# A three-stage fp32 kernel on one core: planned durations set to the trace, and a new table of order and engines

## The chip, the cores and the metric

The kernel runs on one core of a Trainium2 chip. The time is device time in microseconds (us). The kernel before took 601.26 us, the median of three runs (601.25 to 602.89).

## The reference

Three stages follow one another; all tensors are fp32.

```python
# attention: q, k, v of shape (2, 8, 768, 64)
k_sum = k.reshape(B, H, 24, 32, D).max(axis=3)       # a summary of each block of 32 keys
v_sum = v.reshape(B, H, 24, 32, D).mean(axis=3)
scores_l = scale * q @ k.T, kept where |i - j| < 16, else -1e9
scores_s = scale * q @ k_sum.T + log(32)
a = softmax over [scores_l, scores_s]
x = a @ [v, v_sum]                                     # -> 1536 tokens of 512
# first MLP: w_in 512x2048, w_out 2048x512
h = x @ w_in
g = (a0 + a1 h + a2 h^2 + a3 h^3) / (1 + |b0||h| + |b1|h^2 + 1e-6)
x = g @ w_out
# second MLP
h = x @ w_in2;  g = h * cos(h);  out = g @ w_out2
```

## The kernel before

**Work.** The kernel keeps fp32 accuracy on TensorE by splitting operands of the large products into a high and a low part (gh and gl, xH and xL, both halves of a weight tile w) and adding three products: high by high, high by low, low by high. L777 makes a low part (value minus high part), L324, L322 and L327 are the copies and casts on POOL (GpSimd), ACT (ScalarE) and DVE (VectorE); one helper serves each engine, so their lines appear under many tiles.

**Attention.** K of the first batch comes in by pairs of heads (L454), TensorE transposes it (L463, tile ktp), a copy takes it out of PSUM (tile big) and DVE reduces each block to its maximum (L471). Q is transposed likewise (L432 for the first tile, L581 later, tile qtp; the copy goes to qT). For each tile of 128 queries the key windows are gathered into a tile room; L626 computes scores (tile sp, two halves of the tokens' heads in two PSUM tiles, so two tile numbers alternate); L656 on DVE adds the mask, scales and takes the row minimum, one operation (shown as two instructions) for each pair of heads; L660 on ACT takes the exponential and the row sum; L670 and L673 normalise; L687 transposes the weights (ptp to pt); L734 multiplies with the values (avp). L495 is the block maximum for the second batch, whose K tiles L489 transposes.

**The MLPs.** Weights arrive as 64-bit words and DVE rebuilds fp32 from them by integer operations (L760, L764, L768), a tile of 128 x 512 at a time. L864 is the first h product. L1013 to L1041 evaluate the rational function on ACT, DVE and POOL; L1023 is one product in it. L962 is the second h, L1057 to L1069 the cosine. L1106 accumulates the outputs in PSUM (acc), and L1150, L1136, L1159 finish and store them. The accumulators are saved and refilled by copies (acc<-room, room<-acc, part<-acc).

**What sets the order.** The program first lists operations (`P.op`), each with the engines that can do it and a planned duration on each, then `Plan.order` unpacks a table, `ORDER`, which names for each place in the program the operation and its engine. Every engine runs its instructions in that order, and the DMAs that SP (SyncE) issues stand in the table too. The planned durations (the pairs such as `("T", 0.78)` for TensorE, S for SP) set nothing in the built program beside the table: they were the inputs with which the table was found. Dependencies between operations give the waits. So a change of table moves instructions and can change the engine of an elementwise operation; it can't change what is computed.

Of the kernel before, what the change touches and what calls it, by code (L numbers as in the profile page):

```python
# [17 lines left out]
AX = mybir.AxisListType  # L18
# [3 lines left out]
QC = 1.0 + 1e-6  # L22
# [13 lines left out]
for _p, _t in (("AA", .143), ("AP", .17), ("AT", .25), ("AV", .14), ("PA", .08), ("PP", .08), ("PT", .15),  # L36
# [203 lines left out]


def pool(n):
    return Shared(0.2 + n * 0.00207)


MM = 0.2275
SPT = 1.2


@with_exitstack  # L250
def kernel(
    ctx: ExitStack,
# [26 lines left out]
    G = 4  # L279
# [1047 lines left out]
```

## Time and profile before

| | us |
|---|---|
| median of three runs | 601.26 |
| the profiled execution's span, first to last instruction | 599.4 |
| around the span (median minus span) | 1.9 |
| TensorE (PE) busy | 585.9 (98%) |
| DVE busy | 548.4 (92%) |
| ACT busy | 434.1 (72%) |
| POOL busy | 304.3 (51%) |

The profile is a single execution, and its times are counted from the span's start. PE is matmul, PEld the weight load beside it, SPq the queue from which SP issues DMAs. In a timeline a row joins neighbouring instructions of one line, and its bracket says how long the engine had been idle before, and what ended that. The clock that TensorE was granted is 1.00 in every stretch shown.

### The profile page before, as it was taken

To read this page: it belongs to the slowest core of one execution; us is meant where nothing else is said; L and a number is where in the kernel's file an instruction comes from. 1 tells how busy PE (TensorE), PEld (TensorE's weight loads), DVE (VectorE), ACT (ScalarE), POOL (GpSimd) and SP (SyncE) were. 2 spreads that over 40 slices of the span, in tenths; PEclk is the share of its full clock that TensorE was granted. 3 is DMA by queue.
4 is the path that set the end of the run, shared out by engine and by line. 5 is a ranking of instruction groups with operands and counts; after the bars stand their busy time and mean duration, and the time that the engine had idled before them with its cause. 6 is when DMAs were issued, how large, how long until landed. Compare 5 with 4: busy or idle time off the path is not lost.

```text
span 599.4 us, 10933 instructions
## 1 busy us (share of the span) xinstructions
PE 585.9 (98%) x3897; PEld 501.0 (84%) x3897; DVE 548.4 (92%) x1119; ACT 434.1 (72%) x954; POOL 304.3 (51%) x303
## 2 busy tenths in 40 slices
PE   8879999999999999999999999999999999999997
PEld 7568878888888888888888888888989989998996
DVE  4999999979999999998999999999999998887874
ACT  3989999877587756876789897766767566554653
POOL 5587975247537564557577542444355423732130
PEclk9999999999999999999999999999999999999999
DMA  9897874200321313311220112123322331100104
GB/s 264 218 258 192 204 209 120 75 0 2 106 71 37 106 36 105 106 52 56 70 71 1 36 36 71 37 71 104 109 71 70 106 108 36 35 1 1 53 1 158
DMA packets 68862, 51.85 MB, mean 87 GB/s; under 512 B 37304, under 2 KB 63160, under 8 KB 68808
## 3 DMA queue, kind: packets, MB, share of 16 engines
q1 hardware_dynamic: 68664, 51.03, 29.0%
q8 instruction: 30, 0.49, 0.3%
q14 instruction: 24, 0.20, 0.1%
q10 hardware_dynamic: 144, 0.13, 0.1%
HBM read 47.71 MB, written 3.15 MB: 85 GB/s over the span
## 4 chain that ended last, share of the span: by engine, by line
PE 87%; DVE 9%; ACT 2%; DMA 1%; issue 0%; POOL 0%; SPq 0%; POOLq 0%; DVEq 0%; ACTq 0%
PE acc L1106 43%; PE h L864 22%; PE h L962 18%; DVE sc L656 2%; DMA vw<-in_v_dram 1%; PE avp L734 1%; DVE f L764 1%; DVE f L768 1%; PE ptp L687 1%; PE sp L626 1%; PE warm L356 1%; PE ktp L463 1%; DVE f L760 1%; PE vmp L542 0%; DVE big L471 0%
## 5 line engine op out<-in xcount | busy, mean ns | idle before, releaser
L1106 PE MATMUL acc<-gh,w 128*128 128x512 f32 (+1 forms) x416 | 123.1, 378 | 0.0
L1106 PE MATMUL acc<-w,gh 128*128 128x512 f32 x382 | 119.3, 394 | 0.0
L864 PE MATMUL h<-xH,w 128*128 128x512 f32 (+1 forms) x320 | 99.1, 371 | 0.1
L777 POOL TENSOR_TENSOR gl<-te,gh 128x512 fp32r<-128x512 f32 (+1 forms) x48 | 62.7, 1307 | 67.2 <-ACT gh L322 33.5
L1106 PEld LDWEIGHTS acc<-gh,w 128*128 128x128 f32 x416 | 75.3, 188 | 14.9 <-issue 1.5
L1106 PE MATMUL acc<-gl,w 128*128 128x512 f32 (+1 forms) x208 | 77.6, 373 | 0.0
L1106 PEld LDWEIGHTS acc<-w,gh 128*128 128x128 f32 x382 | 66.7, 189 | 9.4
L1106 PE MATMUL acc<-w,gl 128*128 128x512 f32 x191 | 74.3, 389 | 0.0
L1023 POOL TENSOR_TENSOR tu<-tu,tf 128x512 f32<-128x512 f32 (+1 forms) x41 | 51.4, 1255 | 41.2 <-ACT tf L1015 40.9
L777 POOL TENSOR_TENSOR w<-f,w 128x512 fp32r<-128x512 f32 x39 | 54.4, 1397 | 29.5 <-ACT w L322 15.0
L864 PEld LDWEIGHTS h<-xH,w 128*128 128x128 f32 x320 | 58.5, 188 | 10.6 <-DVE big L495 0.3
L864 PE MATMUL h<-xL,w 128*128 128x512 f32 (+1 forms) x160 | 58.9, 368 | 0.0
L864 PE MATMUL h<-big,w 128*128 128x512 f32 x216 | 52.0, 389 | 0.0
L768 DVE SCALAR_TENSOR_TENSOR f<-raw,f 128x512 int32<-128x512 int32 x64 | 48.3, 759 | 0.3
L1013 ACT ACTIVATE tu<-h,co 128x512 f32<-128x512 f32 (+1 forms) x52 | 33.9, 652 | 19.3 <-PE h L864 18.2
L764 DVE SCALAR_TENSOR_TENSOR f<-raw,f 128x512 int32<-128x512 int32 x64 | 47.3, 745 | 0.6
L864 PEld LDWEIGHTS h<-big,w 128*128 128x128 f32 x216 | 40.6, 188 | 8.4
L1106 PEld LDWEIGHTS acc<-gl,w 128*128 128x128 f32 x208 | 39.1, 188 | 7.0
L1106 PEld LDWEIGHTS acc<-w,gl 128*128 128x128 f32 x191 | 35.9, 188 | 7.9
L1057 ACT ACTIVATE tu<-te 128x512 int32<-128x512 f32 x27 | 17.1, 632 | 32.5 <-DVE te L987 32.2
L324 POOL TENSOR_SCALAR w<-f 128x512 fp32r<-128x512 f32 x28 | 20.0, 715 | 39.8 <-DVE f L768 35.1
L1033 ACT ACTIVATE h<-tf 128x512 f32<-128x512 f32 (+1 forms) x52 | 29.6, 570 | 12.0 <-DVE te L1027 10.8
(222 smaller groups left out, 1530.9 us busy)
## 6 DMA issues: line engine op xcount, KB each, us to landing
raw<-in_moe_w_in_dram SPq DMA_DIRECT2D x32, 512.0 KB, 4.6
raw<-in_moe_w_out_dram SPq DMA_DIRECT2D x32, 512.0 KB, 3.4
vw<-in_v_dram SPq DMA_DIRECT2D x24, 192.0 KB, 3.5
qk<-in_q_dram SPq DMA_DIRECT2D x10, 256.0 KB, 5.3
out_dram<-part SPq DMA_DIRECT2D x8, 256.0 KB, 2.8
part<-in_k_dram SPq DMA_DIRECT2D x8, 192.0 KB, 4.8
big<-in_v_dram SPq DMA_DIRECT2D x3, 512.0 KB, 6.7
qk<-in_k_dram SPq DMA_DIRECT2D x6, 256.0 KB, 5.4
```

The costliest lines, as they stand in the source:

```text
L324: nc.gpsimd.tensor_scalar(out=o, in0=i, scalar1=1.0, scalar2=1.0, op0=ALU.mult, op1=ALU.mult)
L656: lambda e, pr=pr, hh=hh, sv=sv, sp=sp: nc.vector.tensor_tensor_reduce(out=sv()[:, pr, :], in0=sp.t[:, pr, :], in1=m.t, op0=ALU.add, op1=A ...
L764: lambda e: nc.vector.scalar_tensor_tensor(out=ft.t.bitcast(I32), in0=lohi()[1], scalar=-0x40000000, in1=ft.t.bitcast(I32), op0=ALU.bitwis ...
L768: lambda e: nc.vector.scalar_tensor_tensor(out=ft.t.bitcast(I32), in0=lohi()[0], scalar=29, in1=ft.t.bitcast(I32), op0=ALU.logical_shift_r ...
L777: lambda e: E[e].tensor_tensor(out=lo(), in0=x(), in1=hi().bitcast(F32), op=ALU.subtract),
L864: nc.tensor.matmul(out=h.t[:, 0:n], lhsT=lt, rhs=rt[:, kk, cs], start=(k0 == 0 and i == 0), stop=(k0 == 2 and i == 5))
L962: nc.tensor.matmul(out=bank.t[:, c], lhsT=lt, rhs=rt, start=start and i == 0, stop=stop and i == 5, skip_group_check=True)
L1013: lambda e: nc.scalar.activation(out=U(), in_=H(), func=ACTF.Square, scale=b1s))
L1023: lambda e: E[e].tensor_tensor(out=U(), in0=U(), in1=Z(), op=ALU.add))
L1033: lambda e: nc.scalar.activation(out=H(), in_=Z(), func=ACTF.Exp, scale=-1.0))
L1057: lambda e: nc.scalar.activation(out=K().bitcast(I32), in_=S_(), func=ACTF.Identity, scale=1.0 / (2.0 * math.pi)))
L1106: nc.tensor.matmul(out=dst, lhsT=lt, rhs=rt, start=(un.start and not have and i == 0), stop=(un.stop and i == 2), skip_group_check=have)
```

## The change

No operation is added or removed: TensorE has 3421 matmuls and SP 142 issues either way. Some eighteen planned durations are set to other values, which by themselves set nothing in the program, and the table is replaced. Its text is unreadable; a line of it stands for the rest.

```diff
 ORDER = (
-    "c-rk)ON?g6RsQOA-*w;jf4}<g{`)o4-P7Zq=^1+-9?wi>?7=wWB#vccTP8ROa%>aJ1|csTD`5dy#8QX>i%1qqK!CD{;t"
+    "c-rk*TaP8zRbKm6wd;OAb?V&voIaO6eL3CJJ>#CtxSh;+7`yGs#P$T65U?F^BqA;b;uwS#WRQ|zDJY0I5)YP~2ozA1AfzZ#q"
...
-MM = 0.2275
-SPT = 1.2
+MM = 0.2267
+SPT = 0.98
...
-            P.op([("S", 0.62)], [], [raw],
+            P.op([("S", 0.58)], [], [raw],
...
-            P.op([("T", 0.78)], [raw], [tp], tr)
+            P.op([("T", 0.67)], [raw], [tp], tr)
...
-        P.op([("T", 0.44)], [raw], [tp], tr)
+        P.op([("T", 0.36)], [raw], [tp], tr)
...
-            P.op([("T", 0.44)], ss, [pp], tr)
+            P.op([("T", 0.355)], ss, [pp], tr)
...
-            P.op([("T", 6 * 0.12)], reads, [bank[half]] + ([hx["b"]] if wn == "11" else []), mm)
+            P.op([("T", 6 * 0.1185)], reads, [bank[half]] + ([hx["b"]] if wn == "11" else []), mm)
```

What the table does is seen in the order of instructions on an engine. Some fifty elementwise operations change engine: DVE makes 22 of the low parts gl<-te where it made 31, POOL 49 where it made 40; L1023 goes from 11 to 6 on DVE and from 41 to 46 on POOL; DVE gets 7 of the high casts of weights (w<-f) that POOL had, and 6 refills of accumulators that ACT had.

**The first matmuls.** On PE at the program's start, before: ktp are transposes of K, qtp of Q, sp scores.

```order
L356 MATMUL warm<-ident 128x128 x8
L463 MATMUL ktp<-ident,part 64x128 x12
L432 MATMUL qtp<-ident,part 64x64 x16
L463 MATMUL ktp<-ident,part 64x128 x30
L432 MATMUL qtp<-ident,part 64x64 x8
L626 MATMUL sp_290<-room,qT_214 64x120
L626 MATMUL sp_292<-room,qT_214 64x120
```

And the same place now:

```order
L356 MATMUL warm<-ident 128x128 x8
L463 MATMUL ktp<-ident,part 64x128 x24
L432 MATMUL qtp<-ident,part 64x64 x16
L463 MATMUL ktp<-ident,part 64x128 x24
L432 MATMUL qtp<-ident,part 64x64 x8
L626 MATMUL sp_308<-room,qT_234 64x120
L626 MATMUL sp_310<-room,qT_234 64x120
```

Twelve more transposes of K stand ahead of the first sixteen of Q, and all 48 are issued before the first score; before, six were left until after the first four scores. To match, SP now issues the small load of the coefficients first, then four parts of K, then both of Q (before: two of K, one of Q, one of K, one of Q).

**The first scores on DVE.** Before, the block reductions (L471) and one sum of values (L514) stand ahead of most of the scores (L656, each with a second instruction that writes mn), and behind them stands a long run of scores:

```order
L656 ISA mn 128x1
L514 TENSOR_TENSOR big<-big 128x8x64
L471 TENSOR_REDUCE big<-ktp 128x12 x2
L656 ISA sc,mn<-sp_290,room 128x120
L656 ISA mn 128x1
L656 ISA sc,mn<-sp_292,room 128x120
L656 ISA mn 128x1
L656 ISA sc,mn<-sp_290,room 128x120
```

Now the reductions are all done before the first score, a copy of qT, which the next scores on PE need, stands amid the scores, and L514 comes twelve scores later:

```order
L471 TENSOR_REDUCE big<-ktp 128x12 x2
L656 ISA sc,mn<-sp_310,room 128x120
L656 ISA mn 128x1
L656 ISA sc,mn<-sp_308,room 128x120
L656 ISA mn 128x1
L656 ISA sc,mn<-sp_308,room 128x120
L656 ISA mn 128x1
L656 ISA sc,mn<-sp_310,room 128x120
L656 ISA mn 128x1
L392 RECIPROCAL co<-co 128x1
L656 ISA sc,mn<-sp_308,room 128x120
L656 ISA mn 128x1
```

The scores of one PSUM tile are now taken as soon as the matmuls that fill it are issued, not after them all.

**The last elementwise work on DVE.** tu and te are values of the second MLP, gh and gl their parts. Before:

```order
L327 CAST gh<-te 128x512
L1061 SCALAR_TENSOR_TENSOR h<-tu,h 128x512
L777 TENSOR_TENSOR gl<-te,gh 128x512
L1069 TENSOR_TENSOR tu<-tu,h 128x512
L327 CAST gh<-tu 128x512
L777 TENSOR_TENSOR gl<-tu,gh 128x512
L327 COPY room<-acc_6862 128x512
L327 COPY room<-acc_6875 128x256
```

And now:

```order
L327 CAST gh<-te 128x512
L1061 SCALAR_TENSOR_TENSOR h<-tu 128x512
L1061 SCALAR_TENSOR_TENSOR h<-tu,h 128x512
L1069 TENSOR_TENSOR tu<-tu,h 128x512
L327 CAST gh<-tu 128x512
L327 COPY room<-acc_6843 128x512
L327 COPY room<-acc_6856 128x256
```

Both last low parts have left DVE; they stand at the end of POOL's order.

## Rows read from the trace of the kernel before

**Rows 1.** The page: span, busy time of each engine, chain of waits.

```profile
span 599.4 us, 10933 instructions
...
PE 585.9 (98%) x3897; PEld 501.0 (84%) x3897; DVE 548.4 (92%) x1119; ACT 434.1 (72%) x954; POOL 304.3 (51%) x303
...
PE 87%; DVE 9%; ACT 2%; DMA 1%; issue 0%; POOL 0%; SPq 0%; POOLq 0%; DVEq 0%; ACTq 0%
```

**Rows 2.** Busy time by stretch: length, PE, PEld, DVE, ACT, POOL, clock, DMA.

```profile
0.00:20.00 20.00, 16.85 (x244) 13.66 (x244) 11.09 (x45) 9.28 (x35) 11.25 (x39) 1.00 0.94 262
20.00:40.00 20.00, 15.92 (x223) 12.07 (x222) 19.77 (x78) 19.33 (x75) 12.95 (x14) 1.00 0.87 218
40.00:50.00 10.00, 9.23 (x138) 7.89 (x139) 10.00 (x45) 9.01 (x36) 7.12 (x9) 1.00 0.93 249
50.00:100.00 50.00, 48.31 (x582) 41.04 (x582) 48.39 (x177) 47.36 (x166) 38.75 (x43) 1.00 0.73 192
100.00:590.00 490.00, 490.00 (x2689) 421.93 (x2688) 456.96 (x774) 347.53 (x645) 234.21 (x202) 1.00 0.19 59
590.00:600.00 10.00, 5.59 (x28) 4.44 (x26) 2.24 (x4) 1.55 (x3) 0.00 (x0) 1.00 0.28 105
```

**Rows 3.** Waits of PE, whole span: line, releaser, us in total, times, longest.

```profile
PE warm L356 <- POOL ident masks.py:199: 1.4, 1, 1.4
PE sp L626 <- ACT room L322: 1.0, 1, 1.0
PE qtp L581 <- DVE te L1041: 1.0, 1, 1.0
```

**Rows 4.** Timelines of PE and DVE, 4 to 22 us: start, length, instruction, idle before.

```profile
4.79 0.42 PE L356 MATMUL warm<-ident 128*128 128x128 f32 x1
...
8.66 0.51 PE L432 MATMUL qtp<-ident,part 64*64 64x64 f32 x10 [0.59 <-ACT qT L322]
...
10.20 1.21 DVE L327 COPY big<-ktp 128x384 f32<-128x384 f32 x2 [1.61 <-PE ktp L463]
...
17.49 0.88 PE L626 MATMUL sp<-room,qT 64*64 64x120 f32 x16 [1.03 <-ACT room L322]
...
18.07 0.28 DVE L656 CUSTOM_DVE_ANT_0 sc<-sp,room 128x120 f32<-128x120 f32 x1 [0.19 <-PE sp L626]
...
18.28 0.28 DVE L656 CUSTOM_DVE_ANT_0 sc<-sp,room 128x120 f32<-128x120 f32 x1
```

**Rows 5.** Groups of DVE by line and shape: busy us, mean ns, idle before.

```profile
L777 DVE TENSOR_TENSOR gl<-te,gh 128x512 fp32r<-128x512 f32 x31 | 21.5, 693 | 0.3
...
L1023 DVE TENSOR_TENSOR tu<-tu,tf 128x512 f32<-128x512 f32 x10 | 7.1, 711 | 0.0
```

**Rows 6.** Groups of POOL by line and shape.

```profile
L777 POOL TENSOR_TENSOR gl<-te,gh 128x512 fp32r<-128x512 f32 x40 | 55.8, 1395 | 67.1 <-ACT gh L322 33.5 <-DVE gh L327 13.3 <-PE h L962 10.7
...
L1023 POOL TENSOR_TENSOR tu<-tu,tf 128x512 f32<-128x512 f32 x34 | 45.4, 1336 | 39.4 <-ACT tf L1015 39.1
```

**Rows 7.** Line L764, ns least, median, most; then POOL and DVE from 338 us.

```profile
L764 DVE SCALAR_TENSOR_TENSOR f<-raw,f x64: 678/688/1223, 23.2 to 525.5; 128x512 int32<-128x512 int32 x64
...
338.49 1.28 POOL L777 TENSOR_TENSOR gl<-te,gh 128x512 fp32r<-128x512 f32 x1 [0.90 <-PE h L864]
...
339.09 1.22 DVE L764 SCALAR_TENSOR_TENSOR f<-raw,f 128x512 int32<-128x512 int32 x1
```

**Rows 8.** Timeline of the end, 575 to 600 us.

```profile
582.97 0.28 PE L962 MATMUL h<-big,pt 128*128 128x256 f32 x1
...
590.58 0.69 DVE L777 TENSOR_TENSOR gl<-tu,gh 128x512 fp32r<-128x512 f32 x1
...
595.31 0.28 PE L1150 MATMUL acc<-w,gl 128*128 128x256 f32 x1
...
595.70 0.42 DVE L327 COPY room<-acc 128x256 f32<-128x256 f32 x1 [1.49 <-PE acc L1150]
...
596.40 0.38 SPq L1159 DMA_DIRECT2D out_dram<-room  x1
```

More of the change, by code (lines that the diff above doesn't have):

```diff
@@ new lines @@
+    "yvL-=m_pTP4b&l!%~gFMYr9b5|V9zIk89B|kt--BaNz@LLR?%#cI|JhgX?%#d_>sxDpPs8%X^Bc>(<@x#fM`CgK<mTd;%>@8"
+    "E*j&!Oyni@5nC<VK{Mq{FGx!*m%l)05o!xhLzB8MC`}D7G{)z{`rpKd;mtK4M9NvF?e&g_^+pnJtKfHN%ba;4j|Gs+<j*gtq"
+    "LDMXn`3vrEs#^-?^6})wvK(Jdp0A#%%8UN`Q|mqG7pJ|Vn02SOi@NTN&u-lw6`k{{D2|FlfWJIB>eSh)dNf;A*>btN=$E5xa"
+    ">St1%aSC4`giKpY`3mrK7O{GxW%Bl7!*aG*O3cJaTc7$H;x_H6b~L02Zu@S-3xvrI(cL1{a5HM;O^|T*Jd-<+nmZH$Nj?Q(b"
+    "s23qs!UeXf<-51@M%PzM}j36SqV4)NQ5YgW!v@b8?5j`QdRC9XZaILg$;w2mZ<zVMocPk)5wP4~NAd*SQozy%cG!8ueVE65$"
@@ new lines @@
+    "tx1n#=-U0#2zo9G+Ct&)e46aFdxbwA?s_;c@0^IYHId~u>qR2F$lmrJD<a`mh`-~FrK=l#LAzSYe8O8l1OLi~3*Y~CNAbj4l"
+    "XaJY4{Ne_zCPEnpL4q2T4NBqTk`tO_7YRTA~CG33oZv(Lle(;53e*(P@{Ho(Lph|!|5i$}{1mNE~6O5hUJ=o9k=k{a@%cqg&"
+    "pA0YJodFLz!*WnbUh$A0CW#lj(ah~@&H*-94Ctx^+zjcn6Gh`q;C<-5{kF&cRRjF91M20u0{Gd_evaQ*IX``a!%u#~12gIxe"
+    ")vP&^v*v(_9f)3{N7|Dp%*lOkzvLPeW&;YcO4Z1I~D#b@G`HD06I|1j>G|39HN`2{TnxUpf}y4pyDNms$!|LS~(1catJ%qK5"
+    "Jl)u~V#+!f{-ODHT4Q+)b34sj12}1K`WJ7xkK^aU2Im37hm~&N*AJ**`WtKz2TkaO5KZB;H352Gt(=pGz4hZjAXDNGOG<Yb}"
@@ new lines @@
+    "b*P28`5@+Scgq^x|e1SetKnNC%D!sH*J-|xJ0;P}9`d>K+H<RcM6G=xjW9z6W~1LGybx>Yj$Abl)QZz3T?&-1%oz0Wa8a7P5"
+    "fN7MrU1vYZsvtQDER~1=NXvOwe90+k!cp4s^@E49RkH-K*3`*s2P$N*QmB8)z&`WeT=HdPU@9jB0hxHoe2@y64NX9CLgM$dN"
+    "u<K+&)tQ2vlrkTL|DyY~kCd(Am~)=WB>53^V-HYwe&EC`{yu;j;t*2w`l4}bq<vLRwazogi6B>sC)rp1!skMVF%Kq=eg`vj="
+    ")pc?4pKqn@=fs(%ANOlS3}QxwT2HqsJr+?DUrRXRKi2i?RMXNmskF0Kg*x2JkTygqn%GXZ(Rmx!h2myx7*FMn_fs+R2M12dv"
+    "-JA9xzwu#|>L|b0>#a;XKLn0>;5WY#`wG!hM{;RO$j`nUh^$=6xR@aQCc+8?MWkn#~mRSCiNWk56YCB&i0MA*<&?o}KN~qKc"
@@ new lines @@
+    "%#lvzt<(oF)-q>9o?oUx%>TP+^c6KD%EN9^OaAIP>|2oB3Y(`>Cov`Gc(wzj_z&Zgmsww7o|VKdYgsoj8CUE?J4ZGWK-B(At"
+    "f5Vg`^?pm@@^JOGd_OY-%+NRFdfkl;4BTSRwB$QW9Fp9>em0vMYiuOp-PPGZ;wo$gB5||i|b;rWb>6ejA*fPb0FYS6^<;*bM"
+    "dPy+b0<Z@P(<1G8s}&wPuTady4HGXVyHzZ{6)`%$T`|%G%37h?mcK0sdqg9px05*&tx{0c@|FXnbL~OIHYiRAwUS9mf^E47d"
+    "oZ$1UTo`dE9{mZ0@?;haM@EK-yUjcJ?+PB8*I-_(#FXwnzru9KBwbr3lGIj2Rs`I;nG&wRmZ1<3bxHFYs0pE*Tl}PtXsijtx"
+    "{6Hg;hJz9?z(FY(Q-ZSy5+n!lJ5a3$T?_GE2;awl3th^N6;NC8I87aW#x0OQvT?1A(OTiTocXiy;m"
@@ L515, in v_mean0 @@
                                                    op=ALU.add))
-            P.op([("T", 0.89)], [raw], [vp],
+            P.op([("T", 0.955)], [raw], [vp],
                  lambda e, i=i, x=x: nc.tensor.matmul(
@@ L720, in attn_c @@
                      prio=P.now - lead)
-            P.op([("S", 1.09)], [], [vw["w"]],
+            P.op([("S", 0.87)], [], [vw["w"]],
                  lambda e, vw=vw, w=ws[half]: nc.sync.dma_start(
@@ L737, in mm @@
                             rhs=pts[hh].t[0:KW, pr, c0:c0 + 64], start=True, stop=True)
-        P.op([("T", 1.1)], pts + [vw[x] for vw in vw2 for x in "mw"], [op], mm)
+        P.op([("T", 1.08)], pts + [vw[x] for vw in vw2 for x in "mw"], [op], mm)
         T, c = divmod(128 * u, TT)
```

90 lines of the change are left out of this document (35 added, 55 removed).

## The prediction

> **What bounds the kernel now.** I read the page first: TensorE is busy for 585.9 of a span of 599.4 us and holds 87% of the chain of waits, DVE 9% [rows 1]. A mean like that hides where the other 13.5 us are, so the next view is busy time by stretch [rows 2]. From 100 to 590 us PE is busy for all of 490.00 us. Nothing that the change does there can gain; it can only open a gap. The idle time lies in front and at the end: 3.15 us up to 20 us, 4.08 from 20 to 40, 0.77 from 40 to 50, 1.69 from 50 to 100, and at the end 4.41 in the last ten microseconds, of which 0.6 lie past the span. In front DVE is busy for 19.77 of 20 us between 20 and 40, for all 10.00 from 40 to 50, and 48.39 of 50 after: while PE waits, DVE works without a gap, so DVE carries the front even where the list of PE's waits names ACT, for ACT waits for DVE. That list [rows 3] shows no single step that would be the cure: behind the first matmul's own 1.4 us the longest waits are 1.0 us each, one for ACT's room and one for DVE's te. Last I read the two timelines of the beginning and the one of the end [rows 4, 8].
>
> So the question is small. The execution profiled has 599.4 us of span, and with the 1.9 us around it that is the median of 601.26. All that could go is the idle time in front, 9.7 us, and of that the first matmul's 1.4 stays [rows 3]. What a measurement of this kernel can tell from no change is about 0.3%, or 1.8 us.
>
> **The change part by part.** Same operations, so the PE work in the sum is unchanged; what moves is who waits.
>
> *First transposes.* Before, the transposes of Q stand on PE behind the first twelve of K and wait 0.59 us for ACT, and DVE behind them sits idle 1.61 us until the next ktp arrives [rows 4]. With 24 transposes of K first, DVE has its next pieces at hand. It can't gain more than the 1.61 us; stepping by hand through the arrivals of the K parts I get 0.9 us, nearest to the middle of 0 and 1.61, and I take that. The coefficients' load, now first on SP, delays each K part by one issue; the warm-up matmuls hide that for the first, the last of them starting at 4.79 us [rows 4]. If the part came later than they end, its delay would show whole, one issue, 0.38 us by the row of the last store [rows 8]; between 0 and 0.38 I take 0.
>
> *First scores.* Here the new order may lose. A score operation on DVE that has to wait for its matmuls comes at most 0.58 us after they began: PE starts the run at 17.49, the waiting score starts at 18.07, and the one behind it 0.21 us later [rows 4]. Before, a long run of scores stood behind the reductions, and matmuls had run ahead of it: one wait of 0.19. Now I find four places where PE must wait for a score or for the copy of qT before its next matmuls, and DVE in turn for those. If nothing overlaps, each round takes 0.58 us plus a hop back of about 0.11 (PE's last matmul ends at 595.59, DVE's copy starts at 595.70, [rows 8]) plus 0.21 for the operation, less the 0.06 of a matmul that runs meanwhile (16 in 0.88): 0.84 us, and four take 3.4. Against the 0.9 us won above that is +2.5 us of DVE time. If PE runs ahead as it did before, nothing is lost and DVE stays 0.9 us ahead. The row of before says that a wait can be as small as 0.19, the other end assumes four full rounds; between −0.9 and +2.5 I take the middle, +0.8. Nothing covers a loss here, as DVE has next to no idle time from 20 us on [rows 2].
>
> *Through the front.* How much later than PE's own work PE runs is set by the DVE work that must precede its matmuls. Adding up mean durations along each order, the tightest early place is the 199th row of DVE's order, a block maximum of the second batch (L495): before PE's work of 46.3 us may go on, DVE must have done 56.1 us before and 56.9 now. That is +0.8 us if DVE is the bound there, and it is [rows 2]. Ends: 0, if PE's next wait takes it up, and +0.8. I take +0.8. From PE work 74 us on the new order asks 1 to 3 us less of DVE. Then the later waits lose their reason: PE's idle time of 0.77 and 1.69 us between 40 and 100 us, 2.46 together [rows 2]. Ends −2.46 and, as some of these waits name ACT and POOL, −1.7. I take −2.1.
>
> *The middle.* DVE loses nine low parts of 693 ns and five products of 711, 9.8 us, to POOL, where they take 1395 and 1336, 19.2 us [rows 5, 6]; some casts and refills come to DVE in return. POOL was busy for 304.3 us [rows 1], and PE is without idle time there: worth 0, bounded by 0 and by one late operation, 0.7 us (1.395 less 0.693), as each such part now ends that much later. The nearest gate between a part and its use is the last, so I price it there.
>
> What POOL does beside DVE is not free: the conversion L764 takes 688 ns as a median and 678 at least, yet 1223 at most, on one and the same shape; the longest, from 339.09 us, lies beside a low part on POOL that began at 338.49 and took 1.28 [rows 7]. The Trainium skill (GPSIMD Engine Reference, 8. Key points) says that GpSimd shares its SBUF interfaces with VectorE and that they contend where a DVE instruction has two SBUF inputs or runs in a 2-port mode; the trace agrees in this one pair of rows. By that rule the added work would lengthen some of DVE's operations. Even if all of the 19 us slowed DVE by the ratio 1223 to 688, DVE would lose 19.2 × 0.44 = 8.4 us over 490 us in which it had 33 us idle [rows 2]; the end would not move.
>
> *The end.* The last h is ready about 2 us of PE work later than before, and the last low part takes POOL's 1.4 us in place of DVE's 0.69. Before, the last h matmul ended at 583.25 and the last low part at 591.27 [rows 8], 8.0 us. Now the part itself takes 0.70 more, and the cast and low part of te no longer stand in its way on DVE; by hand the chain takes 7.4 to 7.5 us, and 7.5 to 7.7 us of PE work stand ahead of its use. Cost 0 to 0.7; I take 0.15. The last store hangs on the same kind of copy as before, 0.42 us after 595.70 and issued at 596.40: 0.
>
> Sum: 0.8 + 0.8 − 2.1 + 0.15 = −0.35 us. Against the median of 601.26 that is 600.9.
>
> **The rivals.**
>
> *The front comes out faster.* DVE wins the 0.9 us of the start, the scores cost nothing, and the waits from 40 to 100 us go: −0.9 + 0.8 − 2.46 = −2.6, so 598.7. For it: DVE is the bound and later places ask less of it. If half of the 4.08 us of idle time between 20 and 40 us goes too, 596.7. Against it: the place at PE work 46.3 asks for more.
>
> *The scores go back and forth.* Slower: four full rounds, +2.5, carried whole by a DVE without idle time up to PE work 46.3, +0.8, while of the later waits only 0.9 us goes as DVE is late: +2.4, and with the end +0.3, 604.0. It decides if DVE ends its first block of scores more than about 1.5 us later than my sum has it. For it: PE and DVE wait for each other in the order itself. Against it: the matmuls of a score are short, and PE had 3.15 us idle up to 20 us that can absorb some.
>
> *The end or the middle stalls.* The low parts on POOL come late: +0.7 once at the end, and once or twice in the middle, 602.0 to 602.7. Against it: the other distances are over a microsecond. It stays within what can't be told from no change.
>
> *The table changes nothing that matters.* PE-bound for 490 us, and a front bound by the same DVE work: within 0.5 us of 601.3. I count this with my forecast, since gains and losses that cancel look the same in time.
>
> **How the numbers follow.** Forecast, with gains and losses cancelling to within 1.8 us: 0.47, by itself 599.5 to 603.0. Faster front: 0.30, nearly all of it past the 0.3%. Back and forth: 0.18, all of it slower. A stall at the end or in the middle: 0.05, of which 0.02 slower by more than 0.3%. That gives faster 0.30, same 0.50, slower 0.20. The range takes in the faster case down to 597.6, halfway between its two times, and the slower one up to its lesser half, 603.6.
>
> **What would show it.** In the profile of the changed kernel: DVE's idle time ahead of its second copy of ktp falls from 1.61 us to under 0.8; DVE's first block of scores has waits on PE of some tenths of a microsecond each, adding up to 1 to 3 us, where there was 0.19; PE's busy time in 50 to 100 us is above 49.5 where it was 48.31; 100 to 590 us shows PE busy throughout; POOL's busy time is above 315 and DVE's below 545. The forecast is wrong if PE has idle time after 100 us, which would mean that a low part on POOL or an accumulator's refill comes late; if the stretch from 20 to 50 us loses much less or more than its 4.85 us; or if the last store is issued more than 1 us later after PE's last matmul than 1.09 us.

## The result, and the profile after

The changed kernel takes 605.32 us, the median of four runs (604.06 to 607.16), against 601.25 of before (599.93 to 602.89, four runs): a ratio of 1.007, 95% interval 1.005 to 1.0089. It is slower, by 4.1 us, and above the range of the prediction, 597.6 to 603.6. The rival in which the scores go back and forth, 604.0, lies nearest.

The page of the kernel after, the lines that answer to [rows 1]:

```profile
span 604.2 us, 10965 instructions
...
PE 588.3 (97%) x3897; PEld 502.9 (83%) x3897; DVE 544.6 (90%) x1102; ACT 428.5 (71%) x955; POOL 322.9 (53%) x319
...
PE 83%; DVE 8%; ACT 3%; DMA 3%; issue 1%; SPq 1%; DVEq 0%
```

The span is 4.8 us longer. PE is busy for 2.4 us more although its matmuls are the same 3897, and the chain of waits has lost four points of PE. More busy time for the same work is the first sign that some of it ran slower. Busy time by stretch (columns as in [rows 2]), kernel after:

```profile
0.00:20.00 20.00, 14.98 (x241) 12.62 (x242) 8.53 (x37) 8.86 (x30) 11.08 (x41) 0.96 0.91 262
20.00:40.00 20.00, 17.57 (x226) 12.54 (x224) 18.92 (x84) 19.02 (x70) 11.62 (x11) 0.96 0.77 197
40.00:50.00 10.00, 7.69 (x81) 6.62 (x85) 9.43 (x36) 6.93 (x24) 6.81 (x8) 0.66 0.91 246
50.00:100.00 50.00, 47.88 (x620) 40.67 (x611) 45.36 (x180) 45.96 (x171) 33.23 (x37) 1.00 0.69 177
100.00:590.00 490.00, 489.90 (x2702) 421.97 (x2697) 457.39 (x763) 343.57 (x656) 257.25 (x221) 1.00 0.20 61
590.00:610.00 20.00, 10.33 (x49) 8.45 (x47) 4.98 (x10) 4.12 (x8) 2.93 (x2) 0.98 0.18 67
```

From 100 to 590 us PE is busy for 489.90 us, where it was 490.00 [rows 2]: the middle costs 0.1. At the end it ran 5.59 us before and 10.33 now, so 4.74 us of its work were still to do at 590 us. Less the 0.1, 4.6 us were lost ahead of 100 us. Two things stand out there. Up to 20 us PE is busy for 14.98 where it was 16.85. And the clock, in the third column from the end, was 1.00 in each of these stretches and is 0.96, 0.96 and 0.66 now.

Waits of PE in the kernel after (columns as in [rows 3]):

```profile
PE sp L626 <- DVE mn L656: 2.2, 4, 0.7
PE sp L626 <- ACT qT L322: 1.7, 2, 0.9
PE qtp L581 <- ACT qT L322: 1.7, 1, 1.7
...
PE ktp L463 <- DMA part<-in_k_dram: 0.9, 1, 0.9
```

The first row isn't in the list of before at all. Matmuls of scores wait for reductions of scores, and these wait for matmuls in turn; DVE's waits in the kernel after:

```profile
DVE sc L656 <- PE sp L626: 4.6, 11, 0.9
```

Five of the eleven, 2.7 us, lie among the first sixteen scores, those of the first two tiles of queries. The same row in the kernel before:

```profile
DVE sc L656 <- PE sp L626: 0.5, 2, 0.3
```

PE's timeline of the first scores, kernel after:

```profile
15.02 0.43 PE L626 MATMUL sp<-room,qT 64*64 64x120 f32 x6 [0.50 <-DVE mn L656]
...
16.60 0.85 PE L626 MATMUL sp<-room,qT 64*64 64x120 f32 x24 [0.69 <-DVE mn L656]
18.03 0.52 PE L626 MATMUL sp<-room,qT 64*64 64x120 f32 x8 [0.59 <-DVE mn L656]
19.02 0.68 PE L626 MATMUL sp<-room,qT 64*64 64x120 f32 x8 [0.47 <-DVE mn L656]
```

And DVE's, of the same stretch:

```profile
14.67 0.28 DVE L656 CUSTOM_DVE_ANT_0 sc<-sp,room 128x120 f32<-128x120 f32 x1
...
15.49 0.28 DVE L656 CUSTOM_DVE_ANT_0 sc<-sp,room 128x120 f32<-128x120 f32 x1 [0.53 <-PE sp L626]
...
18.58 0.28 DVE L656 CUSTOM_DVE_ANT_0 sc<-sp,room 128x120 f32<-128x120 f32 x1 [0.70 <-PE sp L626]
...
19.78 0.28 DVE L656 CUSTOM_DVE_ANT_0 sc<-sp,room 128x120 f32<-128x120 f32 x1 [0.91 <-PE sp L626]
...
22.07 0.28 DVE L656 CUSTOM_DVE_ANT_0 sc<-sp,room 128x120 f32<-128x120 f32 x1
```

Read the two side by side. DVE's reduction ends at 18.58 less 0.70, so at 17.88; PE's next eight matmuls start at 18.03; DVE's next reduction starts at 18.58, 0.55 later; PE starts again at 19.02. Each waits for the other. The last row is the sixteenth score. In the kernel before it started at 20.11:

```profile
20.11 0.28 DVE L656 CUSTOM_DVE_ANT_0 sc<-sp,room 128x120 f32<-128x120 f32 x1
```

Why does a matmul wait for a reduction of other heads? The plan's dependencies are by pair of heads: the matmuls write `sp[y]`, the reduction of pair `pr` reads `sp[pr]`. But the four pairs lie in one PSUM tile, and the waits that the program is built with are by tile. In the plan a matmul of the second pair may run while the first is being reduced; on the chip the trace shows it waiting for that reduction. That the sharing of the tile is what makes it wait was tried (below, two tiles).

The clock, in stretches of one microsecond, kernel after:

```profile
18.00:19.00 1.00, 0.52 (x8) 0.25 (x9) 0.29 (x2) 0.00 (x0) 0.16 (x1) 0.63 1.03 341
19.00:20.00 1.00, 0.98 (x9) 0.48 (x10) 0.22 (x3) 0.00 (x0) 0.00 (x0) 0.50 1.16 292
...
42.00:43.00 1.00, 0.96 (x4) 0.66 (x4) 1.00 (x4) 0.99 (x4) 0.88 (x2) 0.57 1.10 336
43.00:44.00 1.00, 0.10 (x1) 0.00 (x0) 1.00 (x4) 0.97 (x5) 1.00 (x2) 0.50 0.95 219
...
48.00:49.00 1.00, 1.00 (x7) 1.00 (x6) 1.00 (x9) 0.51 (x2) 0.38 (x1) 0.51 0.87 188
```

0.50 is the lower of the two levels, 1.2 GHz. In narrower stretches it is seen to hold from about 18.3 to 21.7 us and from about 42.1 to 49.0. The first fall lies amid the score waits. Ahead of the second, PE had stood still for 1.68 us; a second idle place, of 0.93 us, lies inside the slow stretch. PE's timeline, kernel after:

```profile
41.33 0.66 PE L581 MATMUL qtp<-ident,qk 128*128 128x128 f32 x4 [1.68 <-ACT qT L322]
42.04 1.06 PE L489 MATMUL ktp<-ident,qk 128*128 128x128 f32 x4
44.03 1.89 PE L626 MATMUL sp<-room,qT 64*64 64x120 f32 x32 [0.93 <-ACT qT L322]
```

What the lower clock does to a matmul is seen on L517 (ns least, median, most), kernel after; the most is 1061, and was 610 of the same six before (second row):

```profile
L517 PE MATMUL vmp<-big,vsel x6: 592/682/1061, 19.6 to 22.8; 128*24 128x512 f32 x6
...
L517 PE MATMUL vmp<-big,vsel x6: 592/592/610, 18.3 to 21.2; 128*24 128x512 f32 x6
```

At the end of the kernel after, the last matmul starts at 600.05 and the last store is issued 1.11 us later, which was 1.09 [rows 8]:

```profile
600.05 0.28 PE L1150 MATMUL acc<-w,gl 128*128 128x256 f32 x1
...
601.16 0.41 SPq L1159 DMA_DIRECT2D out_dram<-room  x1
```

So there are two candidates for the loss, both in front: the waits between scores and their reductions, and a TensorE clock that fell twice.

### The profile page after: what moved, and what is told of

Its sections match the earlier page's. It is cut to its first block, busy times and chain, and to the rows that moved or that the text cites. A ratio compares the mean times of both kernels' runs of the same rounds, so it can differ in the third digit from the quotient of the medians.

```text
span 604.2 us, 10965 instructions
## 1 busy us (share of the span) xinstructions
PE 588.3 (97%) x3897; PEld 502.9 (83%) x3897; DVE 544.6 (90%) x1102; ACT 428.5 (71%) x955; POOL 322.9 (53%) x319
## 4 chain that ended last, share of the span: by engine, by line
PE 83%; DVE 8%; ACT 3%; DMA 3%; issue 1%; SPq 1%; DVEq 0%
PE acc L1106 39%; PE h L864 23%; PE h L962 16%; DMA vw<-in_v_dram 2%; PE ptp L687 1%; ACT sc L660 1%; PE sp L626 1%; DVE h L1061 1%; PE avp L734 1%; DMA part<-in_k_dram 1%; PE vmp L517 1%; DVE gl L777 1%; DVE f L768 1%; DVE te L1069 1%; PE ktp L463 0%
## 5 line engine op out<-in xcount | busy, mean ns | idle before, releaser
L777 POOL TENSOR_TENSOR gl<-te,gh 128x512 fp32r<-128x512 f32 (+1 forms) x57 | 75.8, 1331 | 48.5 <-ACT gh L322 24.0
L864 PE MATMUL h<-xH,w 128*128 128x512 f32 (+1 forms) x320 | 99.9, 372 | 0.3 <-DVE big L495 0.2
L1023 POOL TENSOR_TENSOR tu<-tu,tf 128x512 f32<-128x512 f32 (+1 forms) x46 | 56.4, 1229 | 40.4 <-ACT tf L1015 38.6
L777 POOL TENSOR_TENSOR w<-f,w 128x512 fp32r<-128x512 f32 x40 | 56.6, 1418 | 39.7 <-ACT w L322 22.3
L864 PEld LDWEIGHTS h<-xH,w 128*128 128x128 f32 x320 | 58.6, 188 | 11.0 <-DVE big L495 0.4
L864 PE MATMUL h<-xL,w 128*128 128x512 f32 (+1 forms) x160 | 58.9, 368 | 0.0
L864 PE MATMUL h<-big,w 128*128 128x512 f32 x216 | 52.4, 389 | 0.0
L1013 ACT ACTIVATE tu<-h,co 128x512 f32<-128x512 f32 (+1 forms) x52 | 33.9, 653 | 23.2 <-PE h L864 21.7
L768 DVE SCALAR_TENSOR_TENSOR f<-raw,f 128x512 int32<-128x512 int32 x64 | 47.3, 742 | 0.5
L864 PEld LDWEIGHTS h<-big,w 128*128 128x128 f32 x216 | 40.6, 188 | 8.4
L764 DVE SCALAR_TENSOR_TENSOR f<-raw,f 128x512 int32<-128x512 int32 x64 | 45.8, 719 | 0.5
L1064 ACT ACTIVATE h<-h 128x512 f32<-128x512 f32 x48 | 28.2, 587 | 21.1 <-DVE h L1061 20.6
L660 ACT ACTIVATE sc<-sc,mn 128x120 f32<-128x120 f32 x96 | 36.9, 387 | 4.3 <-DVE mn L656 4.2
L1035 DVE SCALAR_TENSOR_TENSOR tu<-tu,h 128x512 f32<-128x512 f32 (+1 forms) x52 | 33.4, 641 | 6.4 <-ACT h L1033 5.1
```

Of the source, the lines that this page charges most:

```text
L660: lambda e, pr=pr, hh=hh, sv=sv: nc.scalar.activation(out=sv()[:, pr, :], in_=sv()[:, pr, :], func=ACTF.Exp, scale=-1.0, bias=mn.t[:, hh, ...
L764: lambda e: nc.vector.scalar_tensor_tensor(out=ft.t.bitcast(I32), in0=lohi()[1], scalar=-0x40000000, in1=ft.t.bitcast(I32), op0=ALU.bitwis ...
L768: lambda e: nc.vector.scalar_tensor_tensor(out=ft.t.bitcast(I32), in0=lohi()[0], scalar=29, in1=ft.t.bitcast(I32), op0=ALU.logical_shift_r ...
L777: lambda e: E[e].tensor_tensor(out=lo(), in0=x(), in1=hi().bitcast(F32), op=ALU.subtract),
L864: nc.tensor.matmul(out=h.t[:, 0:n], lhsT=lt, rhs=rt[:, kk, cs], start=(k0 == 0 and i == 0), stop=(k0 == 2 and i == 5))
L1013: lambda e: nc.scalar.activation(out=U(), in_=H(), func=ACTF.Square, scale=b1s))
```

## Experiments

The table can't be edited by eye, but it can be taken apart: the operations up to some place from the one table, and those that remain in the order of the other. For such kernels the edit says which come from where. Ratios are to the kernel before, on the same chip.

**Front of before, rest of after.** The first 848 places are those of the kernel before (its windows follow that kernel's to 100 us: PE busy for 48.35 us from 50 to 100, where before has 48.31; only from 20 to 40 it has 14.95 for 15.92, with a wait of 1.2 us for a load of q that the profile of before lacks), and the later ones come from the kernel after:

```diff
-ORDER = the table of after
+ORDER = the first 848 of before, then what remains, as it stands in after
```

> The table is the order of before for its first 848 operations (up to the last product with the values, about 124 us) and the order of after for the rest. Theory A (the loss lies in the front: scores and matmuls that wait for each other, and a clock that falls where PE sat idle): as before, 600.5 to 602.5 us, clock 1.00 throughout. Theory B (the loss lies in the rest: low parts moved to POOL, the two gaps of 0.2 us at 404 and 408 us and the end): 604 to 606 us.

Measured: 602.11 us, ratio 1.0012 (0.9996 to 1.0029). It can't be told from the kernel before. The new order of the middle and of the end, with the low parts on POOL, costs little: by the interval at most 1.7 us. The two profiles also show that one and the same front can differ by about 1 us from one execution to another.

**Front of after, rest of before.** The reverse, cut at place 837:

```diff
-ORDER = the table of after
+ORDER = the first 837 of after, then what remains, as it stands in before
```

> The reverse: the first 837 operations in the order of after, the rest in that of before. Theory A: as after, 604 to 606 us, with granted clock 0.5 for some microseconds around 20 and 45 us. Theory B: 600.5 to 602.5 us.

Measured: 606.98 us, ratio 1.009 (1.0069 to 1.0111). The loss lies in the first 837 places, but this kernel loses more than the kernel after, for its seam adds a wait that neither whole kernel has (PE's L864 waits 1.67 us at 130.6 us for DVE's L745). Its six runs fall in two groups: 604.41 and 604.55 at a granted clock of 1.0 as the mean over the run, 606.87 to 608.09 at 0.991 to 0.994. The kernel before, at 0.999 or more on the same chip, took 600.92 as a median of 17 runs. So there is a loss of 3.6 us (604.5 less 600.9) without any clock lost, of which the seam can have up to 1.7, and one of 2.4 to 3.6 more in runs with a lower clock. In the kernel after itself the run at 0.999 took 604.06, those at 0.992 605.88 and 607.16. The mean clock has to be read with care: it takes in the very end of the span, where PE is done, so start of after, rest of before (below) has a mean of 0.997 with 1.00 in every stretch up to 590 us.

**Scores of before, rest of after.** To part the start from what follows, the first 117 places (first transposes and first scores) from before:

```diff
-ORDER = the table of after
+ORDER = the first 117 of before, then what remains, as it stands in after
```

> Only the first 117 operations (up to the end of the first block of scores, about 22 us) are in the order of before, all others in that of after. Theory A1 (the first block of scores alone makes the loss, and what comes later follows from it): 600.5 to 602.5 us. Theory A2 (the stretch of 30 to 60 us has a loss of its own, DVE and ACT orders there): 602.5 to 604.5 us, PE idle again about 2.5 us between 39 and 44 us and the clock down there.

Measured: 609.04 us, ratio 1.0126 (1.0107 to 1.0144). This one tells nothing on the question, for the seam itself made a new wait: PE's transposes L687 wait 5.9 us for a normalisation on POOL (L673) that now stands behind other work, and from 20 to 40 us PE is busy for 12.61 us only, at a clock of 0.83.

**Scores behind their matmuls.** The table of after, with only the reductions (L656) and exponentials (L660) of the first two query tiles moved behind the last score matmul of their tile. PE's and ACT's own orders stay as they are; what changes is which matmuls come behind a reduction of their tile in the program. On DVE, the kernel after with minus, this one with plus:

```
 L471 TENSOR_REDUCE big<-ktp 128x12 x2
+L392 RECIPROCAL co<-co 128x1
+L327 COPY qT_317<-qtp 128x256
 L656 ISA sc,mn<-sp_310,room 128x120
...
-L392 RECIPROCAL co<-co 128x1
 L656 ISA sc,mn<-sp_308,room 128x120
 L656 ISA mn 128x1
-L327 COPY qT_317<-qtp 128x256
```

> The table of after with one thing moved: the 28 or so score reductions and exponentials of the first two query tiles that stood between the score matmuls of their tiles stand behind the last of these matmuls. Theory A1 (PE and DVE wait for each other because each reduction of a PSUM tile stands between matmuls into the same tile): PE's waits on the scores, 2.2 us in 4 places, go to nearly none, and the time falls by 1.5 to 4 us, to 601.5 to 604. Theory A2: the waits at the scores go, yet the time falls by under 1 us, since DVE waits for all matmuls first or the later stretch decides.

Measured: 602.56 us, ratio 1.0023 (1.0011 to 1.0036): 2.8 us of the 4.1 are back. At a clock of 1.0 its runs took 600.85 and 600.91, as fast as the kernel before, and the one at 0.999, which is the one profiled, 602.26. PE's waits in this kernel begin with

```profile
PE sp L626 <- ACT qT L322: 2.1, 2, 1.3
PE qtp L581 <- ACT qT L322: 1.5, 1, 1.5
```

and the row with mn is gone. DVE starts its first score later, at 16.08 instead of 14.67 us, and its sixteenth at 20.36 instead of 22.07:

```profile
16.08 0.28 DVE L656 CUSTOM_DVE_ANT_0 sc<-sp,room 128x120 f32<-128x120 f32 x1
...
20.36 0.28 DVE L656 CUSTOM_DVE_ANT_0 sc<-sp,room 128x120 f32<-128x120 f32 x1
```

Starting each score as soon as it can start costs 1.7 us by the sixteenth. Both falls of the clock are missing from this profile: it is 1.00 in every stretch up to 590 us.

**Scores in two PSUM tiles.** The order of after untouched; the four pairs of heads of the first two query tiles lie in two PSUM tiles in place of one:

```diff
+        alt = [new("pa", [128, NP, KW], F32, f"acc{[(1, 2), (0, 3)][u][hh]}", 1, f"sp{hh}") for hh in range(2)] if u < 2 else sps
+        spt = lambda hh, pr: (alt if (u < 2 and (pr % 2 if u == 0 else pr > 1)) else sps)[hh].t
...
-                            nc.tensor.matmul(out=sps[hh].t[c0:c0 + 64, pr, :],
+                            nc.tensor.matmul(out=spt(hh, pr)[c0:c0 + 64, pr, :],
...
-                         out=sv()[:, pr, :], in0=sp.t[:, pr, :], in1=m.t, op0=ALU.add, op1=ALU.min,
+                         out=sv()[:, pr, :], in0=spt(hh, pr)[:, pr, :], in1=m.t, op0=ALU.add, op1=ALU.min,
```

> The table of after, unchanged; only the scores of the first two query tiles go to two PSUM tiles for each half of the heads where they shared one, so that a matmul of one pair of heads need not wait for the reduction of another pair. Theory A1 (the waits come from sharing the tile, not from the data): the waits of the score matmuls on DVE's reductions, 2.2 us in 4 places, fall to under 1 us with the same order, and the time falls by 1 to 3 us against after's 605.3, to 602.5 to 604.5. Rival (DVE and PE need each other's data in that order): the waits stay, 604.5 to 606.5.

Measured: 603.79 us, ratio 1.0032 (1.0018 to 1.0046). PE has no wait for mn among its scores any more, and the sixteenth score on DVE starts at 19.92 us (lines are two later in this kernel):

```profile
15.58 0.28 DVE L658 CUSTOM_DVE_ANT_0 sc<-sp,room 128x120 f32<-128x120 f32 x1 [0.76 <-PE sp L628]
...
19.92 0.28 DVE L658 CUSTOM_DVE_ANT_0 sc<-sp,room 128x120 f32<-128x120 f32 x1
```

With the same order and the same work this shows that it was the shared tile that made the matmuls wait. On this the Trainium skill (PSUM — Partial Sum Buffer, PSUM bank collisions raise a hardware error) says that two engines must not access one bank and quadrant of partitions at once, and that waits must be set by bank and quadrant, or simply by bank, and not by address. By that rule a finer wait inside one tile was not to be had, as its matmuls and its reductions touch the same partitions; no run here tried one. A second tile was to be had, here in an accumulator's room. The first fall of the clock went with the waits: it is 1.00 from 0 to 20 and from 20 to 40 us, where the kernel after has 0.96 twice. What is left of the loss is the second fall: from 40 to 50 us it is 0.66 as in the kernel after, and eleven of its twelve runs have a mean clock of 0.997 or less; the one at 0.999 took 601.31.

```profile
40.00:50.00 10.00, 8.54 (x117) 7.53 (x117) 8.62 (x35) 6.42 (x23) 5.58 (x7) 0.66 0.90 243
```

**Idle places filled.** The table of after; matmuls near the second fall of the clock are made more than once, into the same places (the first transposes of K of the second batch three times, one block of products with the values twice):

```diff
-            for pr in range(NP):
+            for pr in [x for _ in range(1 + 2 * (i == 0)) for x in range(NP)]:
...
-            for pr in range(NP):
+            for pr in [x for _ in range(1 + (u == 2)) for x in range(NP)]:
```

> The kernel after with two places of idle time on PE filled by repeats of matmuls with the same result: the product with the values of the third query tile is made twice (32 more matmuls, 1.1 us, into an idle time of 1.7 us at 39.7), the first transposes of K of the second batch three times (8 more, 0.7 us, into an idle time of 0.9 us at 43.1). Theory C (the half clock from 42 to 49 us follows from PE sitting idle in these two places, and costs 2 to 3 us): granted clock 1.00 from 40 to 50 us, and 602.5 to 604.5 us. Rival (the clock falls for another reason, or costs nothing as DVE bounds the front): clock down as before or time the same, 604.5 to 606.5.

Measured: 604.29 us, ratio 1.005 (1.003 to 1.007). More work on PE, and a median 1.0 us below that of the kernel after; their intervals overlap, so the profile has to decide. In it the clock is 1.00 from 40 to 50 us, while the score waits are still there:

```profile
40.00:50.00 10.00, 8.53 (x175) 7.46 (x173) 9.96 (x37) 8.51 (x31) 7.12 (x8) 1.00 0.89 247
```

```profile
PE sp L626 <- DVE mn L656: 2.3, 4, 0.7
```

So the waits and the second fall are apart from each other: this edit takes the second fall and leaves the waits, and with them the first fall (0.97 and 0.95 up to 20 and 40 us); the one before did the reverse. At 0.999 and more its runs took 603.9 to 604.25, again some 3 us above the kernel before.

**Copies of qT early.** With the scores behind, PE's longest waits name ACT's copies of qT. Here each is moved four places ahead in ACT's order:

```diff
-ACT: op, op, op, op, copy qT, ..., op, op, op, op, copy qT
+ACT: copy qT, op, op, op, op, ..., copy qT, op, op, op, op
```

> The table of scores_behind, with two copies of transposed Q on ACT moved ahead of 3 and 2 other ACT operations (a coefficient product, exponentials). There PE waited 1.49 and 1.34 us for them at 39 and 41.7 us. Theory A2 (ACT's order there costs time of its own): these waits fall to under 0.6 us each and the time falls by 0.5 to 2 us below scores_behind's 602.6, to 600.6 to 602. Rival (DVE bounds the front there, so the waits only move): 602 to 603, with waits elsewhere grown.

Measured: 603.34 us, ratio 1.003 (1.0017 to 1.0043), no better than without. The waits named qT shrink, and others of the same size come up:

```profile
PE ktp L489 <- DVE te L1041: 1.8, 1, 1.8
...
PE sp L626 <- DVE xL L745: 1.2, 1, 1.2
```

PE needs DVE in the same two places: the transposes L489 start behind DVE's L1041, which ended at 39.61 us without this edit and ends at 39.93 with it, and the next scores behind DVE's L745, at 41.62 and now at 42.13. DVE is later for it waits 0.24 us for ACT's L1015, which the moved copy put off. So in these two places the waits named ACT were DVE's load in another name, as the prediction had it. All eleven runs have a mean clock of 0.997 or less, so the times by themselves don't decide it.

**Start of after, rest of before.** Only the first 54 places from after: the new order of the transposes, without its scores.

```diff
-ORDER = the table of before
+ORDER = the first 54 of after, then what remains, as it stands in before
```

> The first 54 operations (up to the last block reductions, before the first score) in the order of after, all others in that of before. Theory S (after's start is better by up to 0.9 us, as DVE's idle time of 1.61 us falls): 600 to 601 us, ratio to before 0.9985 to 1.000. Rival (the arrival of K sets the start, nothing gained): 601 to 602.5, with DVE idle 2 us and more ahead of its third piece of K as in after.

Measured: 602.47 us, ratio 1.0022 (1.001 to 1.0035), slower than before; yet in the profile PE's last matmul starts at 594.41 us, 0.9 earlier than the 595.31 of [rows 8]. The gain is lost again in the last three microseconds, timeline of this kernel:

```profile
593.65 0.37 ACT L322 COPY room<-acc 128x256 f32<-128x256 f32 x1 [1.13 <-PE acc L1150]
...
594.05 2.52 ACTq L1159 DMA_DIRECT2D out_dram<-room  x1
...
594.41 0.28 PE L1150 MATMUL acc<-w,gl 128*128 128x256 f32 x1
...
596.62 0.58 ACT L322 COPY room<-acc 128x512 f32<-128x512 f32 x1 [2.59 <-issue]
597.65 0.38 SPq L1159 DMA_DIRECT2D out_dram<-room  x1
```

ACT issues one of the last stores, which took it 0.37 us in the kernel before and 2.52 here; its copy of the last room waits 2.59 us behind that, and the last store with it. In the trace's DMA records a queue that loads instructions (8 KB at a time) has a load at 595.04 us here, within the stall and ahead of ACT's last few instructions; in the kernel before that queue's last load is at 585.39. The records don't say for which engine a load is.

**The same with eight small copies on ACT.** If that load is ACT's and makes the stall, more instructions on ACT ahead of it shift it away from the end:

```diff
+        pad = const.tile([128, 1], F32, name="pad")
+        for i in range(8):
+            nc.scalar.copy(out=pad, in_=ident[:, 0:1])
```

> start_after_rest_before with 8 tiny copies more on ACT before its first work, where it is idle. In start_after_rest_before PE ended 0.9 us earlier than in before, but ACT stood 2.59 us behind its own store's issue at the end, and the trace shows a fetch of 8 KB of instructions on queue 14 at 595.04, in that stall; in before the last such fetch is at 585.39. Theory F (ACT waited for its next instructions): with more ACT instructions ahead the fetch comes earlier, the stall goes, the store's issue takes 0.4 us, and the time is 600 to 600.8, 0.5 to 1 us under before's. Rival (the issue itself was slow, as SP issued at the same time): stall and time stay, 602 to 603.

Measured: 603.38 us, ratio 1.0035 (1.0022 to 1.0047), above both expected times. The stall is gone (the last load at 587.62 us, the store's issue 0.37), and the time is no better, for the front became slower: PE waits 1.7 us for qk to be loaded and 1.0 for vw.

**Before with the same eight copies.**

```diff
+        pad = const.tile([128, 1], F32, name="pad")
+        for i in range(8):
+            nc.scalar.copy(out=pad, in_=ident[:, 0:1])
```

> The control: the kernel before with the same 8 tiny copies on ACT. Theory F: they change only where fetches fall; if none falls into the last five microseconds, 600.5 to 602, ratio 0.999 to 1.001. If a fetch does, 2 us more, with ACT idle at the end behind an issue.

Measured: 603.65 us, ratio 1.0044 (1.0029 to 1.0058), where 600.5 to 602 was expected. The copies and their tile make the kernel before 2.5 us slower. PE's waits and the windows of this kernel:

```profile
PE qtp L584 <- DMA qk<-in_q_dram: 2.2, 1, 2.2
```

```profile
20.00:40.00 20.00, 14.27 (x209) 12.12 (x210) 17.57 (x67) 16.24 (x59) 10.68 (x11) 0.91 0.99 216
```

PE was busy for 15.92 us in that stretch at a clock of 1.00 [rows 2]. Eight copies of one column can't take that by their own time, and ACT is busy for less there than before.

**Scores behind, idle places filled.** Both cures at once, the edits of two kernels above together:

```diff
-ORDER = after
+ORDER = after with L656, L660 of the first two query tiles behind their matmuls
-            for pr in range(NP):
+            for pr in [x for _ in range(1 + 2 * (i == 0)) for x in range(NP)]:
```

> scores_behind with the two repeats of idle_filled. In scores_behind the runs at granted clock 1.00 took 600.9 us and those at 0.997 and 0.994 took 601.7 to 604.7. Theory C (what is left of the loss in scores_behind is the clock that falls behind idle PE near 40 us): most runs at clock 0.999 or above, median 600.7 to 601.7, so both halves of the loss are undone. Rival (the repeats cost as much as they give, or the fall has another place): 602 to 603.

Measured: 602.44 us, ratio 1.0022 (1.0011 to 1.0033), as without the repeats. The clock holds (0.999 or more in nine of eleven runs, where it was three of twelve), but the runs at 1.0 now take 601.47 to 603.08 in place of 600.9. It may be that the repeated matmuls cost about what the clock gave back; the spread of those runs is not explained.

**Start of after, ten copies late.** The small copies once more, now at place 2700 of the table, behind almost everything, so that the front's instructions are those of start of after, rest of before:

```diff
-        for o in order:
+        pad = const.tile([128, 1], F32, name="pad")
+        for place, o in enumerate(order):
+            if place == 2700:
+                for _ in range(10):
+                    nc.scalar.copy(out=pad, in_=ident[:, 0:1])
```

> start_after_rest_before with 10 tiny copies more on ACT, placed late (some 40 us before the end), where ACT is idle and the front is not touched. In start_after_rest_before the last fetch of ACT's instructions came behind its 1088th instruction of 1093, at 595.04 in the final stores; with 10 more ahead of the tail it comes about 589 us, in idle time. Theory F with theory S (start of after 0.9 us better, lost to the fetch): ACT's store issue takes 0.4 us, PE ends by 594.7 as it did, and the time is 599.8 to 600.8, ratio 0.998 to 1.0. Rival (the front gain is gone in most runs, or the stall stays): 601.2 to 602.6.

Measured: 603.74 us, ratio 1.0043 (1.0029 to 1.0056), above both expected times. The stall is gone once more, the last load of instructions being at 578.5 us. The store's issue takes 0.37 again. But the front is slow again with not one instruction changed in it. DMA of the first 40 us, this kernel:

```profile
q1 hardware_dynamic: 19342, 9.10, 96.3%
...
raw<-in_moe_w_in_dram SPq DMA_DIRECT2D x4, 512.0 KB, 7.0
```

And of start of after, rest of before:

```profile
q1 hardware_dynamic: 20576, 9.86, 89.7%
...
raw<-in_moe_w_in_dram SPq DMA_DIRECT2D x4, 512.0 KB, 4.9
```

Fewer packets and bytes took the queues longer: 0.963 of 16 engines' 40 us over 19342 packets is 31.9 ns each, against 27.9. What the three padded kernels share and the others lack is the small copies and their four-byte tile `pad`; in the last of them the copies come long after the front, which leaves the tile. That it takes room ahead of other tiles in SBUF, that those moved, and that their loads are slower for it, is a guess: no kernel with the tile and without the copies was run.

## Why the prediction was wrong

The step that failed is **First scores**. The sum has +0.8 us for it, and about 3 were measured at full clock. Between −0.9 and +2.5 us it took the middle, although nothing in the rows of before spoke for the middle. The two ends were two different courses, in one of which PE runs ahead of the reductions and in the other not, and the new order decides between them: a reduction stands behind the first matmuls of its tile, in a tile that the next matmuls write. Working by pairs of heads, as the plan does, one may think that PE runs on; the wait is for the tile. That could have been read from the kernel, where the four pairs are slices of one `sp`. The trace has it four times, 0.47 to 0.69 us of PE each, and 2.7 us of DVE among the first sixteen scores. By the sixteenth score DVE is 1.7 us later than in the same kernel with the scores behind, 2.2 later than with two tiles, and 2.0 later than before. Against the sum, which has DVE 0.8 later, that is 1.2; the rival's point of decision was 1.5, so its sign stayed just short although its loss came. At full clock the waits cost about 3 us: 3.2 in the kernel after (one run at 0.999, 604.06, less 600.9), 2.8 to 3.2 in idle filled, and 3.6 less a seam of up to 1.7 in front of after, rest of before. With the scores behind, −0.1 to 1.3 of it is left, and with two tiles 0.2 in the one run at 0.999. The rival's price for four rounds, 0.84 us each or 3.4, is about that size, though its hop back of 0.11 us was read from PE to DVE, and from DVE to PE the trace has 0.15 (17.88 to 18.03). That the rival's 604.0 lies nearest the time is in part luck: it takes off 0.9 us for the start that doesn't come back, and has no loss of clock.

The second miss is a term that wasn't there: **the clock**. The prediction has the clock at 1.00 in its rows and then nothing on what idle PE might do to it. In the kernel after it is at 0.50 for some 10 us of the profile. The Trainium skill (TensorE: Matmul & The Clock Gate, A second HAM failure mode: psum-queue depth-cycling) tells of a kernel whose clock swings between its two levels because PE idles briefly between groups of matmuls while PSUM tiles are cycled. The trace agrees for the first fall, which begins at 18.3 us between waits of 0.59 and 0.47 and is gone with them in two tiles. Of the profiles of kernels with the scores of after, the three with these waits have this fall (after, front of after, idle filled), and the four without them don't. The lower clock goes with 2.4 to 3.6 us in runs where the mean is 0.991 to 0.994, by front of after, rest of before; with the second fall filled up, the median went down by 1.0, with overlapping intervals. The median of the loss, 4.1 us, is then about 3 of waits and the rest clock. The two can't be added for a single run from what was measured, as part of what runs slowly lies under waits of DVE.

The other steps:

- *First transposes*, 0.9 us: the size came out in one profile (start of after, rest of before: PE ends 0.9 us earlier), though one front can differ by about 1 us between executions, and it doesn't reach the time. In that kernel ACT stalls at the end; in the kernel after nothing of it is left beside the score waits. The sign for it failed, so that the size agrees is no proof of the mechanism: DVE's idle time was to fall from 1.61 to under 0.8 us, and is 2.29 ahead of its second reduction of K, just before the second copy. Part of that is PE's new wait of 0.89 us for a part of K, as the waits of after show above; in start of after, which hasn't this wait, the idle time is still 1.18. The coefficients' load ahead of these parts was priced at 0. It doesn't make the wait by itself: idle filled and start of after issue the same loads in the same order, and PE has no such wait there.
- *Through the front*, +0.8 and −2.1: the 2.1 didn't come. PE is busy for 47.88 us from 50 to 100 where I had asked for more than 49.5, and 48.31 before. Nor is it hidden by the scores alone: with the scores behind their matmuls and at full clock the new order takes 600.85 to 602.26, the time of before or more, and not 2 us less. Summing mean durations along each order found a gain that isn't in the time. Whether the +0.8 is there was not tried by itself.
- *The middle*, 0: right. PE is idle for 0.1 us in all of it, although 316 of the table's 3040 operations name another engine than before; the fifty or so above are what is left when changes to and fro cancel. POOL's busy time is 322.9 us (above 315) and DVE's 544.6 (below 545). The low parts on POOL have the length that was expected (1398 ns, 49 of them); those left on DVE are longer by 0.085 us, at no cost in time:

```profile
L777 DVE TENSOR_TENSOR gl<-te,gh 128x512 fp32r<-128x512 f32 x22 | 17.0, 778 | 0.6 <-ACT gh L322 0.5
```

- *The end*, 0.15: right within what can be seen: PE is busy without a gap from 590 us to its last matmul (10.33 us), and the last store is 1.11 us behind that in place of 1.09.

On the sharing of SBUF between GpSimd and VectorE that the Trainium skill states (GPSIMD Engine Reference, 8. Key points): DVE's low parts went from 693 to 778 ns as POOL got more of them, which agrees (other instances at other places, so it doesn't prove it), and the end did not move, as worked out.

What stays open: why the clock falls in some runs of one kernel and not in others (before has means of 0.991 to 0.997 in 13 of 82 runs, and most of these are 1.5 to 3 us longer); where in the front the part of the 3 us arises that DVE has not yet lost by the sixteenth score; and what makes the loads of the front slower in the kernels with the small copies and their tile. None of the kernels tried beats the one before: the front of before with the rest of after comes nearest, and can't be told from it.

## What to carry to other kernels

An order planned on dependencies finer than the tiles must be read again by tile: a consumer put right behind the first writes of a tile makes the other writes of that tile wait for it, and two engines then take turns. Where PE waits in short rounds, look at the granted clock in narrow windows, for the same matmuls may take nearly twice as long there (592 and 1061 ns here); and where an estimate has two courses with different ends, find what decides between them instead of taking the middle. A stretch to be compared is best shown by splicing: the two tables' halves put the loss in front with one pair of kernels. A splice can add a wait at its seam, so its profile is to be read as well.

## What the runs showed of the hardware that was not expected

- In the kernel after the granted clock fell to 0.50 at 18.3 us, amid waits of 0.47 to 0.69 us, and again at 42.1 us behind one of 1.68; the second time it held until 49.0, though PE was busy without a gap from 45 us on. In scores behind, PE's longest waits are 1.5 and 1.3 us and no stretch of the profile up to 590 us shows a fall, so the length of one wait alone doesn't decide it.
- ACT stalled for 2.59 us at the very end, where a load of instructions fell in that stall. With more small copies on ACT the last such load comes earlier, and the stall is gone: 595.04 us in one kernel, 587.62 with eight copies more and 578.5 with ten. That the load is what ACT waited for is inferred from this.
- Eight copies of one column and one tile of four bytes made the kernel before 2.5 us slower (ratio 1.0044, 1.0029 to 1.0058). Its loads of the first 40 us took longer: 7.8 us to landing in place of 5.5 for the four of raw<-in_moe_w_in_dram. The cause is open.
